# Batch 1's scores in two 64-row bursts, batch 0's output in three parts, and the weight loads in another order, in a one-core attention and mixer kernel

## The chip, the cores and the metric

One core of a Trainium2 chip runs the whole program. The metric is the device time of one execution in microseconds, as the median of repeated runs. Five engines work side by side, each in its own order and held only by semaphores: PE (TensorE, matmuls and transposes), DVE (VectorE), ACT (ScalarE), POOL (GpSimd) and SP (SyncE, which here issues most of the DMAs). POOL issues the weight loads, whose type is changed on the way.

## The reference

Masked attention over 8 batches, 8 heads, 576 positions and 64 features, then two pairs of matmuls:

```
scores = scale * q @ k.T                     # per batch and head
mask: heads 0-3: 0 <= rel < 32;  heads 4-7: 0 <= rel < 128 and rel % 4 == 0
attn = exp(scores) / sum                     # softmax over the allowed keys
x = attn @ v                                 # 576 x 512 per batch
u = x + (relu(x.T @ w_tok1) @ w_tok2).T      # token mixer, 576 -> 256 -> 576
out = u + relu(u @ w_ch1) @ w_ch2            # channel mixer, 512 -> 1536 -> 512
```

Inputs and output are float32 in HBM; the work on the chip is in float16 with float32 sums.

## The kernel before

Batches go through a pipeline. While PE does the channel mixer of batch b (the function `gen_main`), the steps of later batches are put between its matmuls: values and token mixer of batch b+1, scores of batch b+2. `interleave` merges both at build time: each step has a planned time and a cost in planned microseconds, the main generator yields its own costs, and the step with the earliest due time goes next. The result is a fixed order on each engine. The first batches have their times written out by hand at the end of the function (L1006 to L1042).

Names as the profile has them. `l_q`, `l_k`, `l_vn`, `l_vd`, `l_vx`, `l_vt`, `lt` are the float32 loads of a batch (`lt` holds the last 64 rows of q and k); `c_q`, `c_k`, `c_t`, `vv`, `vt` their float16 casts, mostly on POOL. `tp_q`, `tp_k`, `tp_t` are PE transposes into PSUM, copied from there by ACT and DVE into `qz` or `qt` and `kt`, `kr`, `tt`. `sc` and `sm` are score banks; `attp`, `attd` and `attt` the exponentials that ACT writes from them. `av` is the product with v, with the sum of the weights in a 65th column; DVE takes its reciprocal `rec` and writes `xn` (L616, L617). `h1p` and `h1` are the token mixer's hidden layer, `up` and `u16` its result, `tpu` and `uT` that turned over. `gp` and `gt` are the channel mixer's hidden layer in 12 blocks of 128 (L768, weights `w3`), with `gt` L759 for the tail rows; `yp` is its output (L787, weights `w4`), and `o32` the sum that goes to HBM.

Scores come in two forms. In the one-row form (`scores_plain`, `scores_dil`; batches 0 and 1), each head's block is a matmul over 128 rows in which the other head's rows of `qz` are zero, preceded by a matmul of the identity with `veil` (L423) that puts a large negative number where the mask forbids. In the twin form (`scores_twin`, batches 2 to 7), the two heads of a pair use 64 rows each and go side by side; a burst `g` holds two pairs, 24 matmuls on six PSUM banks, and POOL multiplies the exponentials by the mask afterwards. In a batch with twin form the transposes are `bare_steps` (batch 2) or DMAs (batch 3 on).

PSUM has eight banks in three groups: three `main` (gp, yp, gt), two `sc`, three `fl` (transposes, av, h1p, up, tpu). A bank is given anew only when the last reader of its former content is done, so a PE instruction may wait for a copy on ACT or DVE.

Batch 0 has no channel mixer to hide behind: its attention and token mixer run first (L840 to L970). Then come, in program order, the loads of batch 1 behind a small POOL copy that waits for a weight (`gate`, L974), their casts with the last third of `w3` (L984) and all thirds of `w4` (L987 to L990) between, and the loads of batch 2 behind a gate on `w4` (L995). In the channel mixer of batch 0 the output `yp` of a block of 128 rows is summed over all 12 blocks at once (L777 to L804).

Of the kernel before, what the change touches and what calls it, by code (L numbers as in the profile page):

```python
# [20 lines left out]
DM = 512  # L21
# [47 lines left out]
def kernel(  # L69
# [148 lines left out]
    def load_v(b):  # L218
        for step in load_v_steps(b):
            step()  # L220
# [124 lines left out]
    def twinned(b):  # L345
        return b >= 2
# [151 lines left out]
    def scores_twin(b, g):  # L498

        tags = (("sc", 2), ("sc", 2), ("fl", 3), ("fl", 3), ("fl", 3), ("main", 3))  # L500
        if b == 2:
            tags = tags[2:4] + tags[0:2] + tags[4:6]
        ps = [bank(*tags[i], f"sc_{b}_{g}_{i}") for i in range(6)]
        small = ps[4:6]

        def twin(hp, banks, c, keys, queries):
            for h in range(2):
                rows = slice(64 * h, 64 * h + 64)
                n = c.stop - c.start
                nc.tensor.matmul(out=banks[h][:, c], lhsT=keys(rows), rhs=queries(rows), start=True, stop=True)  # L510
# [56 lines left out]
        def mask_tails():  # L567
            t = attt[:, 2 * g:2 * g + 2].rearrange("p a h c -> p (a h) c")[:, :, 64:TW].rearrange(
                "p z (x c) -> p z x c", c=128)[:, :, :, 0:64]
            mult(nc.gpsimd, t, t, tails_seen[g])  # L570

        yield from small_exps(1)
        if b == 2:
            yield from small_exps(0)
        for hp in (2 * g, 2 * g + 1):
            for h in range(2):
                main(hp, h)
                if h and (g or b == 2):
# [3 lines left out]
                yield 0.0  # L582
        if b > 2:
# [145 lines left out]
    def mix_steps(b, t_h1, t_h1b, t_u, t_uT, du=1.0, turn=6.0, gap=2.6):  # L729
# [7 lines left out]
        if turned(b):  # L737
            for t, tail in ((2.0, True), (turn, False))[1 - b % 2:]:
                steps.append((t_u + t * du, 0.0, lambda tail=tail: uT_dma(b, tail)))
            for t, cb in ((0.0, 2), (0.0, 0), (gap, 3), (gap, 1)):  # L740
                steps.append((t_uT + t, 0.0, lambda cb=cb: uT_place(b, cb)))
        else:
            for i, cb in enumerate(CBS):
                steps.append((t_uT + 0.9 * i, 0.28, lambda cb=cb: emit_uT(b, cb)))
        return steps

    def gen_main(b):
# [17 lines left out]
        for mb in range(NMB):  # L765
# [5 lines left out]
            relu(nc.vector if (mb % 2 == 1 if b == 0 else mb % 4 != 3 if b == 1 else mb in (1, 5)) else nc.scalar, gta[:, mb, m0:m0 + 512], p)  # L771
# [5 lines left out]
        for s in ((4, 0, 1, 2, 3) if odd else (0, 1, 2, 3)):  # L777
# [38 lines left out]
    def interleave(main, steps):  # L816
# [3 lines left out]
        while main is not None or steps:  # L820
# [4 lines left out]
            else:  # L825
                try:
                    t += next(main)
# [3 lines left out]
    def warm(n):  # L831

        p = bank("main", 3, "idle_p")
        for _ in range(n):
            nc.tensor.matmul(out=p, lhsT=idle[:, 0:128], rhs=idle, start=True, stop=True)
# [19 lines left out]
    def gate(t, src):  # L855
        nc.gpsimd.tensor_copy(out=t, in_=src)
# [23 lines left out]
    cast_vd(0, 2, nc.gpsimd)  # L880
    load_w3(1)
    cast_vx(0, nc.gpsimd)
# [104 lines left out]
    for i in range(3):  # L987
# [3 lines left out]
    for cast in casts1[12:]:  # L991
        cast()

    new_qk(2)
    gate(l32[(2, "t")][0:1, 0, 0:1], w4[0][0:1, 0:1])  # L995
    for nm in ("q", "k"):
        load_tail(2, nm, nc.sync)
    for h0 in (0, 4):
        for nm in ("q", "k"):
            load_qk(2, nm, h0, h0 + 4, nc.sync)  # L1000
    load_v(2)
# [4 lines left out]
    for b in range(B):  # L1006
        steps = []
        if b == 0:
            steps += score_steps(1, 0, 0, (0.0, 0.7, 1.5),
                                 ((3.0, 5.2), (4.4, 7.0), (7.2, 9.6), (8.6, 11.4)))  # L1010
            va = value_steps(1, 13.4, 0.7)
            steps += va[:4] + [(p + 0.3, c, f) for p, c, f in va[4:]]
            steps += mix_steps(1, 18.0, 20.6, 22.6, 31.4, 1.1)
            steps += at(24.0, 0.3, cast_steps(2))
            bare = bare_steps(2)
            scores2 = score_steps(2, 29.6, 4.4, lag=0.25)
            scores2 = sorted(scores2, key=lambda st: st[0])
            steps += [(t, 0.25, f) for t, f in zip((25.2, 25.9, 27.0, 27.6, 28.2, 34.8, 35.2, 35.6, 36.0), bare)]
            steps += scores2[:10]
            steps += at(34.0, 0.0, [lambda: emit_loads_qk(3)])  # L1020
        elif b == 1:
            va = value_steps(2, 0.0, 1.0)
            steps += [(0.8 + 0.4 * i, c, f) for i, (_, c, f) in enumerate(scores2[10:])]
            steps += [(t, c, f) for t, (_, c, f) in zip((2.2, 3.0, 4.8, 5.6, 8.2, 9.0, 10.4, 11.2), va)]
            steps += mix_steps(2, 7.0, 12.4, 14.6, 24.4, 1.0, 5.6, 0.8)
            casts = cast_steps(3)
            steps += [(6.0 + 0.5 * i, 0.0, casts[i]) for i in (0, 2, 4, 6, 8)]
            steps += [(9.5 + 1.0 * i, 0.0, lambda i=i: cast_qk(3, "q", i, nc.scalar)) for i in range(4)]
            steps += at(11.0, 0.3, casts[9:])
            steps += score_steps(3, 21.0, 4.6, lag=0.1)  # L1030
            steps += at(6.0, 0.0, [lambda: load_v(3)]) + at(20.8, 0.9, load_steps(4))
            steps += at(11.0, 0.9, dma_steps(3)) + at(17.0, 0.4, place_steps(3))
# [40 lines left out]
```

## Time and profile before

| | |
|---|---|
| median of 3 runs | 288.43 us (288.23 to 289.59) |
| the profiled execution | 289.66 us, with a span of 287.8 us |
| PE busy | 276.8 us, 96% of the span |
| ACT, DVE, POOL busy | 134.0, 132.1, 163.0 us |
| granted TensorE clock | 1.00 |
| share of DMA, first 20 us and 20 to 40 us | 1.03 and 1.11 |
| first gp matmul of batch 0 | 28.47 us from the start |
| first yp matmul of batch 0 | 50.38 us |
| first gp matmul of batch 2 | 105.06 us |

A matmul's row has its start and a duration that includes its way through the array (0.38 us for 512 columns), while the next one starts 0.22 us later. So the busy share of PE also covers short waits, and what PE waits is read from the starts of rows.

### The profile page before, as it was taken

The numbers are of one execution on the slowest core, as the hardware profiler recorded it, in microseconds if no ns is written. First come the engines' busy times: TensorE is split into PE (matmuls) and PEld (weight loads), VectorE is DVE, ScalarE is ACT, GpSimd is POOL, SyncE is SP. The second block draws the span as 40 slices with busy tenths as digits, with TensorE's granted clock in tenths as the row PEclk, the third lists the DMA queues.
The fourth block names the chain that finished last, engine by engine and source line by source line (L and its number), as shares of the span: only waits on it lengthen the run. The fifth ranks groups of instructions, "written<-read, shape, count | busy, mean of one in ns | idle before, by whom it ended". The sixth has DMA issues, their size and how long they took to land.

```text
span 287.8 us, 6995 instructions
## 1 busy us (share of the span) xinstructions
PE 276.8 (96%) x2838; PEld 210.9 (73%) x2838; DVE 132.1 (46%) x278; ACT 134.0 (47%) x265; POOL 163.0 (57%) x221
## 2 busy tenths in 40 slices
PE   5879999999999999999999999999999999999995
PEld 2777676888766886698776976797766966886594
DVE  7747658446764236414640164416440274421022
ACT  2854673263543804574447615482546534225500
POOL 6961860478865799449970999279952930000000
PEclk9999999999999999999999999999999999999999
DMA  7999999993999998979888978299974210431023
GB/s 218 263 211 218 283 225 207 320 218 82 328 210 192 264 264 230 139 164 350 226 159 182 330 224 186 57 219 329 193 150 95 85 64 2 91 112 37 0 76 108
DMA packets 105551, 52.63 MB, mean 183 GB/s; under 512 B 73872, under 2 KB 104464, under 8 KB 105520
## 3 DMA queue, kind: packets, MB, share of 16 engines
q1 hardware_dynamic: 101280, 47.07, 67.0%
q0 software_dynamic: 2640, 3.94, 8.0%
q10 hardware_dynamic: 1600, 1.18, 1.4%
q8 instruction: 22, 0.36, 0.6%
q14 instruction: 9, 0.07, 0.1%
HBM read 37.07 MB, written 9.44 MB: 162 GB/s over the span
## 4 chain that ended last, share of the span: by engine, by line
PE 80%; DMA 8%; DVE 3%; POOL 3%; issue 2%; ACT 2%; ACTq 1%; SPq 0%; POOLq 0%; DVEq 0%
PE yp L787 29%; PE gp L768 24%; DMA l_vd<-in_v_dram 4%; PE h1p L627 4%; PE yp L807 3%; DMA l_k<-in_k_dram 3%; PE up L639 3%; PE sc L510 3%; PE gt L759 3%; DVE xn L112 1%; DMA kr<-c_k 1%; PE h1p L625 1%; PE av L608 1%; PE up L650 1%; PE av L603 1%
## 5 line engine op out<-in xcount | busy, mean ns | idle before, releaser
L787 PE MATMUL yp<-w,gt 128*128 128x256 f16 x756 | 87.1, 273 | 0.0
L787 PEld LDWEIGHTS <-gt 128*128 128x128 f16 x768 | 78.6, 106 | 6.5
L106 ACT ACTIVATE gt<-gp 128x512 f16<-128x512 f32 x69 | 41.2, 597 | 76.3 <-PE gp L768 76.0
L768 PE MATMUL gp<-utd,w 128*128 128x512 f16 x144 | 54.7, 380 | 0.0
L768 PE MATMUL gp<-utm,w 128*128 128x512 f16 x144 | 54.6, 379 | 0.0
L768 PEld LDWEIGHTS <-w 128*128 128x128 f16 x384 | 39.2, 114 | 20.3 <-issue 0.5
L797 DVE TENSOR_TENSOR o<-yp,u 128x512 f32<-128x512 f32 x31 | 21.4, 691 | 63.1 <-PE yp L787 58.5
L112 POOL TENSOR_TENSOR attp<-attp,const 128x1280 f16<-128x1280 f16 x12 | 31.4, 2616 | 27.5 <-ACT attp L534 27.4
L112 DVE TENSOR_TENSOR xn<-av,rec 128x320 f16<-128x320 f32 x64 | 31.4, 491 | 2.2
L112 POOL TENSOR_TENSOR attd<-attd,const 128x1024 f16<-128x1024 f16 x12 | 25.3, 2132 | 1.6 <-ACT attd L534 1.6
L768 PE MATMUL gp<-uT,w 128*128 128x512 f16 x96 | 25.8, 379 | 0.0
L108 DVE TENSOR_SCALAR gt<-gp 128x512 f16<-128x512 f32 x27 | 18.5, 686 | 13.6 <-PE gp L768 13.1
L645 DVE TENSOR_TENSOR u<-up,xn 128x512 f16<-128x512 f32 x26 | 17.9, 690 | 7.5 <-PE up L639 7.5
L534 ACT ACTIVATE attp<-sc 128x480 f16<-128x480 f32 (+1 forms) x36 | 16.1, 536 | 7.4 <-PE sc L510 7.4
L102 POOL CAST c_k<-l_k 128x512 f16<-128x512 f32 x29 | 18.0, 628 | 1.9 <-DMA l_k<-in_k_dram 1.7
L102 POOL CAST c_q<-l_q 128x512 f16<-128x512 f32 x27 | 16.8, 629 | 3.1 <-DMA l_q<-in_q_dram 3.1
L616 DVE RECIPROCAL rec<-av 128x5 f32<-128x5 f32 x64 | 12.2, 190 | 13.8 <-PE av L613 13.7
L106 ACT ACTIVATE h<-h1p 128x256 f16<-128x256 f32 x29 | 11.1, 384 | 14.5 <-PE h1p L627 14.1
L399 POOL COPY kt<-kr 128x512 f16<-128x512 f16 x10 | 10.7, 1075 | 9.0 <-DMA kr<-c_k 9.0
L697 ACT COPY utd<-utm 128x512 f16<-128x512 f16 x12 | 12.8, 1135 | 4.1 <-DMA utm<-u 4.1
L102 POOL CAST vv<-l_vn 128x256 f16<-128x256 f32 x32 | 12.0, 420 | 4.3 <-DMA l_vn<-in_v_dram 4.1
L112 POOL TENSOR_TENSOR attt<-attt,const 128x512 f16<-128x512 f16 x12 | 14.0, 1165 | 0.0
(147 smaller groups left out, 459.9 us busy)
## 6 DMA issues: line engine op xcount, KB each, us to landing
out_dram<-o SPq DMA_DIRECT2D x72, 128.0 KB, 3.1
l_q<-in_q_dram SPq DMA_DIRECT2D x15, 512.0 KB, 7.2
l_k<-in_k_dram SPq DMA_DIRECT2D x14, 512.0 KB, 7.1
l_vn<-in_v_dram SPq DMA_DIRECT2D x32, 128.0 KB, 6.6
l_vd<-in_v_dram SPq DMA_DIRECT2D x16, 256.0 KB, 4.6
w<-in_moe_w_ch_dram POOLq DMA_DIRECT2D x6, 512.0 KB, 7.6
lt<-in_q_dram SPq DMA_DIRECT2D x8, 128.0 KB, 4.6
l_vt<-in_v_dram SPq DMA_DIRECT2D x8, 128.0 KB, 4.9
```

The costliest lines, as they stand in the source:

```text
L102: eng.tensor_copy(out=out, in_=in_)
L106: nc.scalar.activation(out=out, in_=in_, func=AF.Relu)
L108: eng.tensor_scalar_max(out=out, in0=in_, scalar1=0.0)
L112: eng.tensor_tensor(out=out, in0=x, in1=y, op=ALU.mult)
L534: nc.scalar.activation(out=out, in_=in_, func=AF.Exp, scale=0.125)
L616: nc.vector.reciprocal(out=rec[:, :, 0], in_=av[:, :, 64])
L627: nc.tensor.matmul(out=p, lhsT=w[:, s, j], rhs=x[:, s, c], start=False, stop=(s == 3))
L645: nc.vector.tensor_tensor(out=u16(b, s), in0=blocks4(p), in1=blocks4(xn[b][:, s]), op=ALU.add)
L697: nc.scalar.copy(out=natural(uTd[:, cb - 2]), in_=uTm[i][:, cb].rearrange("p r m -> p m r"))
L768: nc.tensor.matmul(out=p, lhsT=w3_block(cb, mb), rhs=uT[(b, cb)][0], start=(i == 0), stop=(i == 3))
L787: nc.tensor.matmul(out=p[:, c], lhsT=gta[:, mb, a0:m0 + 512:4] if half else gta[:, mb, a0:a0 + 128], rhs=w4[mb][:, c], start=(mb == 0), st ...
L797: nc.vector.tensor_tensor(out=blocks4(o32), in0=blocks4(p), in1=u16(b, s), op=ALU.add)
```

## The change

- The loads: POOL casts `vt` of batch 0 before it issues the second third of `w3`, and issues the last third right behind it. Batch 1's v loads go in another order. The first third of `w4` is issued behind the casts of batch 1's k; the other two thirds come later, after the first mask and two casts of v. Batch 2's loads no longer wait for `w4`.
- Batch 1 takes the twin form: `bare_steps` for its transposes, two bursts. The second burst has the veil (20 matmuls of 128 columns with the identity), the first is masked by POOL. ACT casts two blocks of `c_q`, DVE casts `vd` and `vx` of batch 1.
- Batch 0's output: blocks 0 to 2 are held in the three `main` banks and summed in three parts of four hidden blocks, with planned times 20.3 and 23.0 for the second and third. Block 3 follows as before. In the hidden layer of batch 0, blocks 0 to 7 are all handed to DVE.
- Six matmuls on `idle` (no result) are put in, three at a time, and the steps of batches 1, 2 and 3 have other times: the scores of batch 2 start behind the first gp of batch 1.

The core of the diff:

```diff
     def twinned(b):
-        return b >= 2
+        return b >= 1
...
         tags = (("sc", 2), ("sc", 2), ("fl", 3), ("fl", 3), ("fl", 3), ("main", 3))
-        if b == 2:
+        if b <= 2:
             tags = tags[2:4] + tags[0:2] + tags[4:6]
...
+        veils = b == 1 and g == 1
...
+        if veils:
+            for p in ps:
+                for r in range(4 if p not in small else 2):
+                    nc.tensor.matmul(
+                        out=p[:, 128 * r:128 * r + 128], lhsT=ident,
+                        rhs=veil[:, BLK + 128:BLK + 256] if p in small else veil[:, 0:128],
+                        start=(r == 0), stop=False)
...
-            relu(nc.vector if (mb % 2 == 1 if b == 0 else mb % 4 != 3 if b == 1 else mb in (1, 5)) else nc.scalar, gta[:, mb, m0:m0 + 512], p)
+            relu(nc.vector if (mb < 8 or mb % 2 == 1 if b == 0 else mb % 4 != 3 if b == 1 else mb in (1, 5)) else nc.scalar, gta[:, mb, m0:m0 + 512], p)
...
+        if b == 0:
+            ps3 = [bank("main", 3, f"yp_{b}_{s}") for s in range(3)]
+            for i in range(3):
+                if i:
+                    yield ("from", (20.3, 23.0)[i - 1])
+                for s, p in enumerate(ps3):
+                    for half in range(2):
+                        c = slice(256 * half, 256 * half + 256)
+                        for mb in range(4 * i, 4 * i + 4):
+                            nc.tensor.matmul(
+                                out=p[:, c],
+                                lhsT=gta[:, mb, s:512:4] if half else gta[:, mb, 128 * s:128 * s + 128],
+                                rhs=w4[mb][:, c], start=(mb == 0 and not half), stop=(mb == NMB - 1 and bool(half)))
...
-        for s in ((4, 0, 1, 2, 3) if odd else (0, 1, 2, 3)):
+        for s in ((4, 0, 1, 2, 3) if odd else (0, 1, 2, 3) if b else (3,)):
...
     cast_vd(0, 2, nc.gpsimd)
+    cast_vx(0, nc.gpsimd)
     load_w3(1)
-    cast_vx(0, nc.gpsimd)
+    load_w3(2)
...
-    load_v(1)
-    casts1 = cast_steps(1)
-    for i in (0, 1):
-        casts1[i]()
-    load_w3(2)
-    for i in (2, 3, 4, 5, 7, 6, 8, 9, 10, 11):
-        casts1[i]()
...
+    load_v(1, (5, 6, 7, 0, 1, 2, 3, 4))
...
+    for i in (0, 1, 3, 2, 4, 6, 8):
+        casts1[i]()
+    load_w4(0)
+
+    def rest1():
+        for i in (9, 10):
+            casts1[i]()
+        load_w4(1)
+        load_w4(2)
+        for i in (11, 12, 13):
+            casts1[i]()
...
         if b == 0:
-            steps += score_steps(1, 0, 0, (0.0, 0.7, 1.5),
-                                 ((3.0, 5.2), (4.4, 7.0), (7.2, 9.6), (8.6, 11.4)))
-            va = value_steps(1, 13.4, 0.7)
...
+            steps += [(t, 0.25, f) for t, f in zip((4.2, 5.4, 7.0, 6.2, 7.6, 11.4, 12.2, 11.8, 12.6), bare)]
+            steps += score_steps(1, 8.9, 4.3, lag=0.25)
+            steps += [(8.6 + 0.6 * i, 0.0, lambda i=i: cast_qk(1, "q", 2 + i, nc.scalar)) for i in range(2)]
+            steps += at(9.0, 0.0, [loads2]) + at(10.8, 0.0, [rest1])
...
+                      zip((16.2, 16.8, 17.5, 18.1, 18.8, 19.4, 21.4, 22.0), (4, 5, 6, 7, 0, 1, 2, 3))]
+            steps += mix_steps(1, 23.2, 20.0, 25.4, 30.2, 1.0, gap_uT=0.8)
+            steps += [(t, 0.0, lambda: warm(3, "sc", 2)) for t in (19.8, 21.3)]
...
-            steps += scores2[:10]
...
         elif b == 1:
             va = value_steps(2, 0.0, 1.0)
...
+            steps += scores2
```

More of the change, by code (lines that the diff above doesn't have):

```diff
@@ L216, in load_v_steps, with load_v @@
         return steps
-    def load_v(b):
-        for step in load_v_steps(b):
-            step()
+    def load_v(b, order=range(8)):
+        steps = load_v_steps(b)
+        for i in order:
+            steps[i]()
     def load_steps(b):
@@ L504, in scores_twin @@
         small = ps[4:6]
+        veils = b == 1 and g == 1
         def twin(hp, banks, c, keys, queries):
+            ends = c.stop == (512 if banks is not small else 256)
             for h in range(2):
                 rows = slice(64 * h, 64 * h + 64)
-                n = c.stop - c.start
-                nc.tensor.matmul(out=banks[h][:, c], lhsT=keys(rows), rhs=queries(rows), start=True, stop=True)
+                nc.tensor.matmul(out=banks[h][:, c], lhsT=keys(rows), rhs=queries(rows),
+                                 start=not veils, stop=ends or not veils)
+        if veils:
[5 more added lines that the diff above has]
+                        start=(r == 0), stop=False)
         for j in range(2):
@@ L577, in scores_twin @@
                 main(hp, h)
-                if h and (g or b == 2):
+                if h and b == 1 and hp == 0:
+                    mask(0)
+                    mask_tails(0)
+                elif h and (b == 2 or (g and b > 2)):
                     mask(hp)
@@ L582, in scores_twin @@
                 yield 0.0
+        if b == 1 and g == 0:
+            mask(1)
+            mask_tails(1)
         if b > 2:
```

79 lines of the change are left out of this document (48 added, 31 removed).

## The prediction

> **What bounds the kernel now.** I read the page first: the busy line and the chain that ended last.
>
> ```profile
> PE 276.8 (96%) x2838; PEld 210.9 (73%) x2838; DVE 132.1 (46%) x278; ACT 134.0 (47%) x265; POOL 163.0 (57%) x221
> ...
> PE 80%; DMA 8%; DVE 3%; POOL 3%; issue 2%; ACT 2%; ACTq 1%; SPq 0%; POOLq 0%; DVEq 0%
> ```
>
> PE sets the end; no other engine is over 57%. So a change is worth the PE work that it removes, plus the waits of PE that it removes, less those that it makes. Next, PE's timeline, at three places that both kernels have, and PE's rows in the list of waits:
>
> ```profile
> 28.47 3.48 PE L768 MATMUL gp<-uT,w 128*128 128x512 f16 x14
> ...
> 50.38 0.82 PE L787 MATMUL yp<-w,gt 128*128 128x256 f16 x6
> ...
> 105.06 0.38 PE L768 MATMUL gp<-utd,w 128*128 128x512 f16 x1
> ```
>
> ```profile
> PE av L611 <- POOL vt L102: 1.2, 1, 1.2
> ...
> PE h1p L625 <- DVE xn L112: 0.4, 1, 0.4
> PE sc L510 <- POOL kt L399: 0.2, 1, 0.2
> ```
>
> From batch 2's first gp (105.06) on, the order is the old one, so the change is decided before it. For the work in between I need the pitch of a matmul, from chain and timeline:
>
> ```profile
> 122.45 0.75 PE sc L510 x24
> ...
> 126.58 0.67 PE sc L510 x24
> ...
> 138.66 0.90 PE gt L759 x16
> ...
> 258.13 3.45 PE gp L768 x16
> ...
> 273.76 9.17 PE yp L787 x84
> ```
>
> ```profile
> 34.30 0.23 PE L423 MATMUL sc<-veil,const 128*128 128x160 f16 x1
> ...
> 34.44 0.23 PE L423 MATMUL sc<-veil,const 128*128 128x160 f16 x1
> ...
> 42.89 0.19 PE L423 MATMUL sm<-veil,const 128*128 128x64 f16 x1
> ...
> 43.09 0.19 PE L425 MATMUL sm<-qz,kt 128*128 128x64 f16 x1
> ```
>
> That is 0.216 for 512 columns, 0.109 for 256, 0.056 for 128, 0.07 for 160 (two steps in 0.14), 0.03 for 64 (seven steps in 0.20). Between 28.47 and 105.06 stand 108 matmuls of 512 columns with their 4 in up (112: 24.2), 268 of 256 (29.2), 140 transposes and gt of 128 (7.8), 120 av of 65 columns (3.6), batch 1's scores (4.9, below) and four bursts (2.8): 72.5 of 76.6. PE waits only 4.1 here, in many pieces; some 1.0 of it are pieces that the new order keeps, 3.1 belong to the old order and go.
>
> **The change part by part.** All times are microseconds.
>
> *The head.* POOL's order around `vt`, before and then after (`w3_1`, `w3_2` are thirds of the first weight):
>
> ```order
> L102 CAST vv0_69<-l_vd_0_123 128x4x2x64 x2
> L860 DMA w3_1_85<-in_moe_w_ch1_dram 128x4x512
> L102 CAST vt0_71<-l_vx_0_124 128x4x64
> L883 DMA w1t1_80<-in_moe_w_tok1_dram 64x256
> L885 COPY w2p_0_82<-w2_81 128x512
> L885 COPY w2p_1_83<-w2_81 128x512
> ```
>
> ```order
> L102 CAST vv0_69<-l_vd_0_123 128x4x2x64 x2
> L102 CAST vt0_71<-l_vx_0_124 128x4x64
> L908 DMA w3_1_85<-in_moe_w_ch1_dram 128x4x512
> L908 DMA w3_2_86<-in_moe_w_ch1_dram 128x4x512
> L932 DMA w1t1_80<-in_moe_w_tok1_dram 64x256
> L934 COPY w2p_0_82<-w2_81 128x512
> L934 COPY w2p_1_83<-w2_81 128x512
> ```
>
> The cast moves ahead of one DMA issue, and one issue more stands ahead of the `w2p` copies. In the trace:
>
> ```profile
> 19.08 0.63 POOL L102 CAST vv<-l_vd 128x512 f16<-128x512 f32 x1 [1.91 <-DMA l_vd<-in_v_dram]
> 19.65 0.74 POOL L860 DMA_DIRECT2D w<-in_moe_w_ch_dram  x1
> 20.38 0.42 POOL L102 CAST vt<-l_vx 128x256 f16<-128x256 f32 x1
> ...
> 21.25 1.25 POOL L885 COPY w2p<-w 128x512 f16<-128x512 f16 x2
> ```
>
> ```profile
> 25.96 0.38 PE L949 MATMUL up<-h,w2p 128*128 128x256 f16 x2
> ```
>
> PE's 1.2 wait for `vt` ends one issue earlier: -0.7, and all that follows up to gp with it. The `w2p` copies end 0.8 later, near 23.3, and PE's first use of them at 25.96 becomes 25.3: still covered, nothing.
>
> *PE's work.* Batch 1's scores were 24 matmuls of 160 columns, 40 of 128, 32 of 64: 1.7 + 2.2 + 0.9 = 4.9. Two bursts cost 0.75 + 0.67, the veil of the second 20 x 0.056 = 1.1: 2.5. That is -2.3. Six idle matmuls: +1.3. The thirds of yp and the transposes are as many as before. Together -1.0.
>
> *New waits, first stretch (to the second third of yp).* They come from order and banks. DVE's order at batch 1's keys, before and after (`gt` is the relu, `kt`, `kr` key copies):
>
> ```order
> L108 TENSOR_SCALAR gt_93<-gp_0_3_677 128x512
> L314 COPY kt_65<-tp_k_1_0_695 128x512
> L102 COPY qz_64<-tp_q_1_1_701 64x576 x2
> L102 COPY kt_65<-tp_q_1_1_701 128x64
> L314 COPY kt_65<-tp_k_1_1_724 128x512
> L108 TENSOR_SCALAR gt_93<-gp_0_5_713 128x512
> ```
>
> ```order
> L386 COPY kt_65<-tp_k_1_0_688 128x512
> L108 TENSOR_SCALAR gt_93<-gp_0_7_685 128x512
> L386 COPY kt_65<-tp_k_1_1_697 128x512
> L108 TENSOR_SCALAR gt_93<-gp_0_9_767 128x512
> L388 COPY kr_67<-tp_k_1_2_810 128x512
> L389 COPY kt_65<-tp_k_1_2_810 128x128
> L388 COPY kr_67<-tp_k_1_3_817 128x512
> L389 COPY kt_65<-tp_k_1_3_817 128x128
> ```
>
> The key copies of a whole burst now stand close together, and the burst needs both. Durations, and how closely ACT follows a burst that PE left at 61.19:
>
> ```profile
> L108 DVE TENSOR_SCALAR gt<-gp 128x512 f16<-128x512 f32 x27 | 18.5, 686 | 13.6 <-PE gp L768 13.1
> ...
> L385 DVE COPY kt<-tp_k 128x512 f16<-128x512 f16 x2 | 1.4, 686 | 0.4 <-PE tp_k L378 0.4
> L387 DVE COPY kr<-tp_k 128x512 f16<-128x512 f16 x2 | 0.8, 420 | 0.2 <-PE tp_k L378 0.2
> ...
> L388 DVE COPY kt<-tp_k 128x128 f16<-128x128 f16 x2 | 0.6, 280 | 0.0
> ```
>
> ```profile
> 61.38 0.38 ACT L534 ACTIVATE attp<-sc 128x256 f16<-128x256 f32 x1 [1.79 <-PE sc L510]
> ...
> 62.46 1.53 ACT L534 ACTIVATE attp<-sc 128x480 f16<-128x480 f32 x3
> 63.81 0.76 ACT L100 COPY uT<-tpu 128x640 f16<-128x640 f16 x1
> ```
>
> Four small exponentials take 1.08 from start to start, a large one 0.45; an engine starts 0.2 behind PE. The second key copy ends 0.2 + 3 x 0.65 = 2.1 after the first tp_k; PE is there after half a gp, a tp_k, a gp and half a burst, 1.8: wait 0.3. All three `fl` banks are held by the burst, so the next transposes wait for ACT's exponentials, behind a cast and four small ones: 0.2, 0.3, and 0.1 for a veil. The last tp_k takes over the bank of the one just ahead of it: 0.2 + 0.42 + 0.28, about 0.9. Together 1.5 to 1.8; I take 1.8.
>
> Then the heads. DVE needs 0.63 a head:
>
> ```profile
> 45.05 0.49 DVE L112 TENSOR_TENSOR xn<-av,rec 128x320 f16<-128x320 f32 x1
> ...
> 45.68 0.49 DVE L112 TENSOR_TENSOR xn<-av,rec 128x320 f16<-128x320 f32 x1
> ```
>
> Before, a gp of 0.43 or more stood between two heads. Now heads 5, 6, 7, 0, 1 follow each other at 0.17 to 0.27, and with three banks the last three wait 0.2, 0.45 and 0.35. The first head waits 0.3 for POOL, whose order has the mask of the first burst ahead of the last v cast. Together 1.3. Bounds of the stretch: 1.4 to 4.
>
> *New waits, second stretch (to 105).* tpu and the transposes of batch 2 now follow each other without yp between: one waits for a bank that ACT empties with the 0.76 copy (0.5), others 0.1 and 0.3 for DVE. Batch 2's first burst comes behind gp 0 of batch 1, and its last tp_k waits for eight exponentials and a copy: 0.2 + 1.1 + 1.8 + 0.6 against 3.2 of PE work: 0.5. Values of head 0 and 1 then wait for POOL's masks and for ACT: 0.7.
>
> ```profile
> L112 POOL TENSOR_TENSOR attp<-attp,const 128x1280 f16<-128x1280 f16 x12 | 31.4, 2616 | 27.5 <-ACT attp L534 27.4
> ...
> L112 POOL TENSOR_TENSOR attt<-attt,const 128x512 f16<-128x512 f16 x12 | 14.0, 1165 | 0.0
> ```
>
> Both h1p pairs come half a gp behind their last head, where DVE needs 0.97 for one and 1.6 for two: 0.5 each. Together 3.1, bounds 1.5 to 4.
>
> *The loads.* w4's first third is issued near 38, when the last load of k, pushed back by up to 3 by w3's last third, is cast; the other two behind the first mask, its tails and two casts of v (2.6 + 0.6 + 0.8 from about 41.3), near 45.5 and 46; PE wants them near 45, 53 and 57.5. Rows of before on them, and on a v load issued right behind a third of w3 (issued at 30.76):
>
> ```profile
> 39.20 1.61 POOL L988 DMA_DIRECT2D w<-in_moe_w_ch_dram  x3
> ```
>
> ```profile
> DMA to landing us min/median/max: 5.5/7.4/10.6
> ```
>
> ```profile
> DMA to landing us min/median/max: 7.8/7.8/7.8
> ```
>
> ```profile
> 38.85 0.41 POOL L102 CAST vv<-l_vn 128x256 f16<-128x256 f32 x1 [2.39 <-DMA l_vn<-in_v_dram]
> ```
>
> The first two answers are for the three thirds of w4 and for the third of w3. The w3 part landed at 38.6, and the v load, a quarter of its size, right after it and not before: that looks like order of issue. But w4's thirds landed some 2.4 and 3.7 apart, the last with batch 2's loads beside it, so loads also share. The Trainium skill ("DMA: Bandwidth & Descriptors", section "Queues, rings and completion order") says that each DMA engine takes turns between the queue rows that have work, packet by packet. By that rule w4 isn't held back by q and k, and the sum stands as below; by order of issue it is the first rival. I take sharing: the second third lands 5.5 + 1.3 after 45.5, near 52.3, and costs nothing; bounds 0 to 1.9. Batch 1's c_t and c_q come up to 3 later behind w3's last third, about when PE wants them: 0, at most 0.9.
>
> *The sum.* -0.7 - 1.0 + 3.1 + 3.1 - 3.1 (old waits) = +1.4. It is a difference within one profiled execution (289.66, of which 287.8 is span); that one lies 1.2 above the median, 288.43, on which I lay it: 289.8, rounded down to 289.7 as neighbouring waits take from each other.
>
> **The rivals.** *The second weight arrives late (slower).* SP has issued four loads of batch 2, 512 KB each, when POOL reaches the second third of w4.
>
> ```profile
> 53.56 0.61 POOL L102 CAST c_q<-l_q 128x512 f16<-128x512 f32 x1 [0.58 <-DMA l_q<-in_q_dram]
> 55.13 0.61 POOL L102 CAST c_k<-l_k 128x512 f16<-128x512 f32 x1 [0.96 <-DMA l_k<-in_k_dram]
> ```
>
> They land 1.5 apart. In order of issue they are through near 52, the third lands near 54.6, and PE has waited since 52.9: +1.7, so 291.4. For it: the v load above. It decides from the point where the landing passes 53.
>
> *The new waits are no more than the old (faster).* If ACT and DVE run ahead enough that 3.1 of new waits replace 3.1 of old ones, the head and the shorter scores remain: 286.7. For it: waits of 0.3 shift each other, and the old order, as dense, has just 4.1. Against: the bank behind the last tp_k, 0.63 a head and the h1p pairs are bound by durations; the 0.4 of h1p in the list of waits is such a case.
>
> **How the numbers follow.** 0.5% is 1.4, about what a measurement here tells from no change: 287.0 and 289.9 are its ends. My forecast has 0.50, with an own range of 288.7 to 290.7: 0.31 within the ends and 0.19 above. The late weight has 0.16, all above. Waits as before: 0.27, of it 0.21 below 287.0. What is left, 0.07, is spread: 0.01, 0.03, 0.03. So faster 0.22, same 0.40, slower 0.38. The range from 286.6 to 291.6 takes in both rivals' times.
>
> **What would show it.** In the profile after: the first gp near 27.8; two bursts of 24 matmuls more and two rows of `idle_p` x3 near 52; PE waiting for DVE before the last tp_k of batch 1 (0.9) and among the heads of batch 1; the second third of yp near 53; batch 2's first gp near 106.5. I am wrong if the second third starts before 51.5 or after 54.5, or if batch 2's first gp comes before 104.5.

## The result and the profile after

The change makes the kernel slower: 293.5 us (median of four; 291.81 to 297.87) against 288.36, ratio 1.0156 with a 95% interval of 1.0125 to 1.0186. Six more runs, later, gave 1.0182 (1.0151 to 1.0213). One run of each set (297.9 and 297.8) had a lower clock and is left out of the ratio, as are, further down, two of e1 (the profiled one among them) and one each of e3, e7, e13 and e14. The forecast was 289.7.

The profiled execution of after took 292.5 (span 290.73), that of before 289.66 (287.82). The page of after, its busy line and the engines' shares of the chain that ended last:

```profile
PE 277.3 (95%) x2816; PEld 209.5 (72%) x2816; DVE 133.5 (46%) x279; ACT 134.2 (46%) x267; POOL 166.0 (57%) x217
...
PE 78%; DMA 11%; POOL 3%; ACT 2%; DVE 2%; issue 1%; ACTq 1%; SPq 1%; POOLq 0%
```

PE is as busy as before; what grew is the share of the DMA in the chain, from 8% to 11%. PE's timeline of after, at the places that the prediction named (start, length, group, and in brackets the idle time ahead with what ended it):

```profile
26.67 4.56 PE L787 MATMUL gp<-uT,w 128*128 128x512 f16 x19
...
53.75 1.03 PE L813 MATMUL yp<-w,gt 128*128 128x256 f16 x8 [1.26 <-DMA w<-in_moe_w_ch_dram]
...
107.38 0.38 PE L787 MATMUL gp<-utd,w 128*128 128x512 f16 x1
```

So 28.47 became 26.67 for the first gp, and 105.06 became 107.38 for batch 2's first. The difference in span, +2.91, is -1.80 up to the first gp, **+4.12 from there to batch 2's first gp** (76.59 to 80.71), +0.20 to batch 3's (28.70 to 28.90) and +0.39 behind it, all behind the last output's landing. The second third of yp starts at 53.75, inside the bounds of the forecast, but for the wrong reason: PE stood there and waited. The list of PE's waits from the first gp to batch 2's:

```profile
PE yp L813 <- DMA w<-in_moe_w_ch_dram: 1.3, 1, 1.3
PE av L622 <- ACT attt L546: 0.8, 1, 0.8
PE tp_k L379 <- DVE kt L389: 0.8, 1, 0.8
PE h1p L644 <- DVE xn L112: 0.8, 2, 0.4
PE av L622 <- DVE xn L112: 0.4, 2, 0.2
PE tp_k L379 <- ACT qt L384: 0.3, 1, 0.3
PE tp_q L379 <- ACT uT L100: 0.3, 1, 0.3
```

Six of the seven rows are waits that the prediction priced, five at about their sizes and one (batch 1's heads, `av` from `xn`) at less. The first is the one it priced at 0. The trace of the loads that write `w`, for the two thirds that POOL issues at 44.4 and 45.0:

```profile
  PE yp L813: 1.3, 1
...
DMA to landing us min/median/max: 9.3/10.2/11.2
```

They take 9.3 and 11.2 and land at 53.7 and 56.1; the thirds of before took 5.5 to 10.6. The DMA view tells why. Three stretches of 1.5 after the issue at 44.4 (q1 carries SP's loads, q0 POOL's; packets, MB, share of 16 engines), from 47, from 48.5 and from 50:

```profile
q1 hardware_dynamic: 527, 0.52, 109.7%
...
q0 software_dynamic: 61, 0.25, 82.0%
q1 hardware_dynamic: 155, 0.15, 33.3%
...
q0 software_dynamic: 65, 0.27, 87.2%
q1 hardware_dynamic: 65, 0.06, 15.4%
```

Until 48.5 not one packet of w4 moves (nor in e9, a second profile of after): the loads that SP issued first, of tails, q and k, go through alone. From then on the two queues take turns, 65 packets against 65, as the Trainium skill's rule has it ("DMA: Bandwidth & Descriptors", section "Queues, rings and completion order"). So both rules that the prediction set against each other held here, one after the other: order of issue for 4 us, then turns. The DMA engines are full throughout; the windows of after show it (the column ahead of the last is their share):

```profile
26.67:53.75 27.08, 24.08 (x256) 15.77 (x254) 16.98 (x38) 11.53 (x25) 17.14 (x24) 1.00 1.14 269
...
51.20:54.60 3.40, 2.13 (x30) 1.65 (x29) 1.70 (x5) 0.00 (x0) 1.56 (x3) 1.00 1.07 233
```

### The profile page after: what moved, and what is told of

It is laid out like the page before. It is cut to its first block, busy times and chain, and to the rows that moved or that the text cites. A ratio compares the mean times of both kernels' runs of the same rounds, so it can differ in the third digit from the quotient of the medians.

```text
span 290.7 us, 6955 instructions
## 1 busy us (share of the span) xinstructions
PE 277.3 (95%) x2816; PEld 209.5 (72%) x2816; DVE 133.5 (46%) x279; ACT 134.2 (46%) x267; POOL 166.0 (57%) x217
## 4 chain that ended last, share of the span: by engine, by line
PE 78%; DMA 11%; POOL 3%; ACT 2%; DVE 2%; issue 1%; ACTq 1%; SPq 1%; POOLq 0%
PE yp L834 26%; PE gp L787 25%; PE up L658 4%; PE gt L778 4%; PE yp L854 4%; PE h1p L646 4%; DMA w<-in_moe_w_ch_dram 3%; DMA l_k<-in_k_dram 3%; PE sc L513 3%; DMA l_q<-in_q_dram 3%; DMA l_vx<-in_v_dram 2%; PE yp L813 2%; PE h1p L644 1%; ACT attp L546 1%; PE av L622 1%; PE up L669 1%
## 5 line engine op out<-in xcount | busy, mean ns | idle before, releaser
L834 PE MATMUL yp<-w,gt 128*128 128x256 f16 x684 | 77.6, 273 | 0.0
L834 PEld LDWEIGHTS <-gt 128*128 128x128 f16 x696 | 71.4, 106 | 5.5
L106 ACT ACTIVATE gt<-gp 128x512 f16<-128x512 f32 x65 | 39.0, 600 | 64.9 <-PE gp L787 64.6
L112 POOL TENSOR_TENSOR attp<-attp,const 128x1280 f16<-128x1280 f16 x14 | 36.6, 2612 | 38.0 <-ACT attp L546 28.2
L787 PE MATMUL gp<-utm,w 128*128 128x512 f16 x144 | 54.6, 379 | 0.0
L844 DVE TENSOR_TENSOR o<-yp,u 128x512 f32<-128x512 f32 x28 | 19.4, 692 | 61.1 <-PE yp L834 50.8
L108 DVE TENSOR_SCALAR gt<-gp 128x512 f16<-128x512 f32 x31 | 21.3, 688 | 12.4 <-PE gp L787 12.0
L546 ACT ACTIVATE attp<-sc 128x480 f16<-128x480 f32 (+1 forms) x42 | 18.7, 538 | 14.1 <-PE sc L513 14.0
L787 PE MATMUL gp<-uT,w 128*128 128x512 f16 x96 | 24.7, 380 | 0.0
L112 POOL TENSOR_TENSOR attt<-attt,const 128x512 f16<-128x512 f16 (+1 forms) x14 | 15.2, 1085 | 0.0
L546 ACT ACTIVATE attd<-sc 128x512 f16<-128x512 f32 x28 | 14.4, 613 | 0.0
```

Source lines behind the costliest of these rows:

```text
L106: nc.scalar.activation(out=out, in_=in_, func=AF.Relu)
L108: eng.tensor_scalar_max(out=out, in0=in_, scalar1=0.0)
L112: eng.tensor_tensor(out=out, in0=x, in1=y, op=ALU.mult)
L546: nc.scalar.activation(out=out, in_=in_, func=AF.Exp, scale=0.125)
L787: nc.tensor.matmul(out=p, lhsT=w3_block(cb, mb), rhs=uT[(b, cb)][0], start=(i == 0), stop=(i == 3))
L834: nc.tensor.matmul(out=p[:, c], lhsT=gta[:, mb, a0:m0 + 512:4] if half else gta[:, mb, a0:a0 + 128], rhs=w4[mb][:, c], start=(mb == 0), st ...
```

## The experiments

Theory **loads without slack** (in the first expectations, "late weight"): the order's own waits are about what was forecast; the new order wants the second weight 4 us earlier against the first gp (yp starts at 44.25, 17.6 behind it; before, 21.9) and its second third comes late. Rival **order and banks**: the waits of the new order make the loss, and PE's wait for the weight covers others of its size. Their time against before is a ratio with its interval. The table holds what PE's timeline shows of each profiled execution: the first gp, the stretch to batch 2's first gp (the one in dispute), and from there to batch 3's. Over the stretch in dispute two executions of one kernel differ by 1.1 (before) and 0.4 (after).

| kernel | first gp | to batch 2 | to batch 3 | ratio |
|---|---|---|---|---|
| before | 28.47 | 76.59 | 28.70 | |
| before again (e8) | 26.66 | 77.66 | 28.70 | |
| vt first (e4) | 26.83 | 76.51 | 28.70 | 0.9997 (0.9983-1.0012) |
| after | 26.67 | 80.71 | 28.90 | 1.0156 (1.0125-1.0186) |
| after again (e9) | 26.73 | 80.33 | 28.88 | 1.0182 (1.0151-1.0213) |
| w4 early (e1) | 27.14 | 84.53 | 33.83 | 1.0316 (1.0276-1.0356) |
| no idle (e2) | 26.93 | 82.60 | 29.24 | 1.0162 (1.0122-1.0203) |
| both (e3) | 27.78 | 82.02 | 29.50 | 1.0283 (1.0242-1.0323) |
| w4, then batch 2 (e5) | 27.30 | 79.63 | 33.21 | 1.0174 (1.0136-1.0212) |
| thirds amid heads (e6) | 28.54 | 79.39 | 29.41 | 1.0145 (1.0118-1.0172) |
| fewer waits (e7) | 26.98 | 78.94 | 29.28 | 1.0105 (1.0083-1.0128) |
| batch 4's loads early (e10) | 26.63 | 81.19 | 31.12 | 1.0269 (1.0247-1.0292) |
| that, loads by need (e11) | 27.99 | 79.29 | 31.15 | 1.0211 (1.0186-1.0236) |
| fewer waits, w4 at start (e12) | 38.02 | 75.98 | 28.82 | |
| loads by need (e13) | 26.77 | 76.90 | 29.89 | 1.0005 (0.9987-1.0024) |
| and q1 later (e14) | 26.79 | 76.79 | 29.55 | 1.0044 (1.0025-1.0064) |
| after, w4 at start (e15) | 37.10 | 79.20 | 33.18 | |
| before, w4 at start (e16) | 39.10 | 76.36 | 28.69 | |
| by need, burst earlier (e17) | 26.82 | 76.53 | 28.75 | 1.0012 (0.9995-1.0029) |
| and sc banks (e18) | 26.74 | 76.95 | 28.99 | 0.998 (0.9958-1.0002) |

**The weight early (e1).**

```
     load_w4(0)
+    load_w4(1)
+    load_w4(2)
...
-        load_w4(1)
-        load_w4(2)
```

> The kernel after, with all three thirds of the second weight issued by POOL behind each other where now only the first is (near 37.4); the casts and masks behind them stay in order. Theory 'late weight': in the profile of after PE waits 1.43 for the second third, issued at 44.4 and landed at 53.7. Issued near 38 it lands near 47, and that wait goes. What is late next is DVE, which finishes heads 2 and 3 of batch 1 near 53.4 where PE would want them for h1p near 53.0: 0.6 comes back, 0.2 more is gained as POOL's last v cast comes earlier (POOL idles 2.25 ahead of its first mask, so the two issues cost it nothing). In sum 1.0 to 1.1 less than after, ratio to before 1.012; up to 2 less (1.009) if the weight comes later still in the timed runs than in the profiled one. Rival 'order and banks' (the loss is made of the waits of the new order, and PE's wait for the weight covers one for DVE of the same size): the ratio stays at 1.0145 to 1.0156.

The wait for w4 went, and 4.0 came in its place. PE's waits, how long v's tail took that SP issued 0.2 behind the first third, and the windows (length, then PE's busy time; the third column from the right is the granted clock):

```profile
PE av L632 <- POOL vv L102: 4.0, 1, 4.0
...
DMA to landing us min/median/max: 12.2/12.2/12.2
...
48.10:51.50 3.40, 0.24 (x3) 0.24 (x3) 0.01 (x1) 0.00 (x0) 0.90 (x2) 1.00 1.12 257
51.50:54.90 3.40, 3.25 (x42) 2.58 (x41) 2.94 (x10) 0.00 (x0) 3.40 (x3) 0.50 1.10 349
...
130.00:133.40 3.40, 1.12 (x26) 0.86 (x27) 0.00 (x0) 0.00 (x0) 3.05 (x5) 1.00 0.88 176
133.40:136.80 3.40, 3.40 (x18) 2.43 (x17) 0.00 (x0) 3.06 (x8) 0.46 (x1) 0.50 0.95 188
```

Both theories missed. A third of w4 gained is a load of v lost, since the engines are full; and a stretch of 3.4 in which PE is idle enough is followed by 3.4 at half clock. That is a price which no part of the prediction had. The two low stretches start 81.9 apart, 24 times 3.41, as if the clock were set anew at fixed times. It fits the Trainium skill ("TensorE: Matmul & The Clock Gate", section "Part 1: The HAM clock gate (the "warmup" mystery)"), which gives a free-running window of 3413 ns.

**Without the idle matmuls (e2), and with both edits (e3).**

```
-            steps += [(t, 0.0, lambda: warm(3, "sc", 2)) for t in (19.8, 21.3)]
```

> The kernel after without the two rows of three idle matmuls (1.29 of PE work, near 49.4 and 51.1). Theory 'late weight': PE comes to the second third of yp 0.8 to 1.3 earlier and waits that much longer for its weight, which still lands near 53.7: within 0.2 of after, ratio to before 1.015 to 1.0165. Rival 'PE work and order' (PE sets this stretch): 0.8 to 1.3 less than after, ratio 1.011 to 1.013.

> Both edits at once. Theory 'late weight': with the weight there, DVE's heads (0.63 each) set the stretch: heads 2 and 3 come 0.8 earlier to PE but wait for banks, h1p half 1 waits 0.5 for head 7: some 0.5 less than with the early weight alone, ratio to before 1.010 to 1.011. Rival 'PE work and order': the same as without idle matmuls alone, 1.011 to 1.013.

For e2 the theory's number came: 1.29 of PE work less, and the same time. But its profiled execution (295.0) shows a longer wait (1.9) and then half clock:

```profile
50.90:54.30 3.40, 1.52 (x27) 1.18 (x25) 2.27 (x8) 0.38 (x1) 2.52 (x5) 1.00 1.06 229
54.30:57.70 3.40, 3.40 (x17) 2.43 (x17) 0.00 (x0) 0.39 (x1) 0.50 (x1) 0.50 1.10 300
```

PE was busy for 1.52 of 3.40 here and for 2.13 in the row of after above, which stays at full clock. The Trainium skill ("TensorE: Matmul & The Clock Gate", section "Why this matters for your kernels") advises against idle gaps over some 3 us. Here one of 1.9 with others beside it was enough, so the busy share of the stretch tells more than its longest gap. In this execution the idle matmuls were missed. That they keep after at full clock is not shown: two of e2's six executions have a mean clock of 0.994, which is one stretch of 3.4 at half clock (1.7 of some 294), and so have two of after's ten. e3 is e1 again, with the wait for v's tail at 2.9, outside both expectations.

**The head (e4, e8).** e4 is before with the cast ahead of one issue; e8 is before unchanged.

```
     cast_vd(0, 2, nc.gpsimd)
+    cast_vx(0, nc.gpsimd)
     load_w3(1)
-    cast_vx(0, nc.gpsimd)
```

> The kernel before with one edit: POOL's cast of vt stands ahead of its issue of the first weight's second third (the third third stays where before has it). Prediction's term: PE's wait for vt ends 0.7 earlier and all behind it moves by that: ratio to before 0.9975. Rival 'the head gives all that the two profiles show' (first gp at 28.47 before, 26.67 after): 1.8 less, ratio 0.994. Rival 'cover': what comes behind (the first weight's thirds, the loads of batch 1) is late next and nothing is gained: 0.999 to 1.001.

> The kernel before, unchanged, for a second profile. In the profile shown the first gp of before stood at 28.47, with the vt cast moved ahead (a run of its own) at 26.83, and yet the two take the same time (0.9997). Theory 'a slow head in that one execution': here the first gp stands near 27.0, and the span from there to batch 2's first gp is again 76.6 within 0.3. Rival 'the cast gains 1.6 at the head and loses it behind': the first gp stands near 28.4 again.

The cast's move is worth nothing (0.9997). PE's waits of e8 from 14 to 30, POOL's row of the cast there, and PE's first gp:

```profile
PE sc L425 <- DVE kt L314: 0.2, 1, 0.2
PE up L949 <- ACT h L106: 0.2, 1, 0.2
...
18.59 0.41 POOL L102 CAST vt<-l_vx 128x256 f16<-128x256 f32 x1 [0.78 <-DMA l_vx<-in_v_dram]
...
26.66 3.48 PE L768 MATMUL gp<-uT,w 128*128 128x512 f16 x14
```

The 1.2 that PE waited for `vt` isn't there. In the execution first shown, half of `vd` landed at 19.0 and held POOL for 1.9 (its row is in the prediction); here both halves are there by 16.5, and the cast waits for its own load whichever side of the issue it stands on. Theory "a slow head" holds for the first gp, but not for the stretch: e8's is 1.1 longer. Batch 1's first q lands 2.9 behind the first gp there, and 1.6 behind it in the execution first shown and in e4; PE then waits for casts of q and k (0.5 in its list).

**The weight ahead of batch 2's loads (e5), yp amid the heads (e6), fewer waits (e7).**

```
         load_w4(2)
+        loads2()
...
         new_qk(2)
+        gate(l32[(2, "t")][0:1, 0, 0:1], w2p[1][0:1, 0, 0:1])
...
-            steps += at(9.0, 0.0, [loads2]) + at(10.8, 0.0, [rest1])
+            steps += at(10.8, 0.0, [rest1])
```

e6 leaves the idle matmuls out and lays the second third earlier; e7 adds a bank:

```
-                    yield ("from", (20.3, 23.0)[i - 1])
+                    yield ("from", (18.0, 21.6)[i - 1])
...
-            p = bank("fl", 3, f"tp_{nm}_{b}_{hp}", FP16)
+            p = bank(*(("sc", 2) if (nm, hp) == ("k", 3) else ("fl", 3)), f"tp_{nm}_{b}_{hp}", FP16)
```

e6 also spreads the heads (16.2 to 21.2) and moves the first h1p pair to 20.9; e7 moves batch 2's heads 0 to 3 by 0.4 to 0.9 and its h1p and up steps by 0.6 to 1.1.

> The kernel after, with batch 2's loads on SP held back until POOL has issued the second weight's second and third third (near 45.5, as late as in the kernel before); POOL's order of casts, masks and w4 stays, with one small copy more. In the early-weight run v's tail (issued by SP 0.2 behind the first third) landed at 50.5 behind all three thirds and PE waited 4.2 for it; here it keeps its place. Theory 'late weight': of the 1.43 that PE waited at the second third of yp nothing is left, as the third lands near 48.5; 0.6 comes back at h1p, which waits for DVE's heads 2 and 3: 0.8 less than after's profile (292.5), and no stretch of 3.4 at half clock any more: ratio to before 1.010 to 1.012. Rival 'order and banks': PE's wait turns into others of the same size, here or at batch 2's transposes, whose loads come later: 1.0135 to 1.0156.

> As the last, and without the six idle matmuls, and with the second third of yp laid between heads 7, 0, 1, 2, 3 and the first h1p pair, where after has heads close together. Theory 'late weight': once the weight is there by 48.5, yp fills what DVE needs for a head (0.63), so that the 0.96 of waits between heads, the 1.29 of idle matmuls and h1p's 0.6 go: 2.2 to 2.8 less than the last, ratio to before 1.002 to 1.005. Rival 'order and banks': DVE and ACT set this stretch whatever PE does between: not under 1.009.

> As the last, with the last key transposes of batches 1 and 2 in a bank of their own (the sc pair in place of fl), batch 2's heads 0 to 3 a gp or half a gp later, and its h1p and up steps 0.6 to 1.1 later. If the waits that PE shows in the profile of after are each worth their length: 0.97 + 0.50 (last tp_k), 1.0 (first head of batch 2, behind its second burst), and most of 0.55 + 0.56 (h1p) go: 2.0 to 2.9 less than the last, ratio 0.992 to 0.998, the first version ahead of before. If such waits only move on to the next step: within 0.5 of the last, 1.001 to 1.005.

In e5 the disputed stretch became 1.1 shorter, near what the theory said (0.8), and the time did not. In the profiled execution, the longest of six (296.4), batch 4's keys came late and half clock followed. The other five (292.6 to 294.3) have mean clocks of 0.998 to 1.000, so no whole stretch at half clock; what held them isn't shown.

```profile
PE sc L513 <- POOL kt L400: 2.5, 2, 1.5
...
124.89:128.29 3.40, 1.37 (x28) 1.08 (x29) 0.00 (x0) 0.23 (x1) 3.04 (x5) 1.00 0.88 173
128.29:131.70 3.41, 3.41 (x19) 2.42 (x17) 0.19 (x1) 2.84 (x8) 0.71 (x1) 0.50 0.92 185
```

e6's stretch is 0.2 shorter where 2.2 to 2.8 were expected, and e7's time another 0.4%, between its two expectations. In e7's list the waits for DVE and ACT that were aimed at are gone or small, and PE, earlier at yp, waits for its weight twice:

```profile
45.66 2.35 PE L813 MATMUL yp<-w,gt 128*128 128x256 f16 x20 [1.24 <-DMA w<-in_moe_w_ch_dram]
...
50.35 1.03 PE L813 MATMUL yp<-w,gt 128*128 128x256 f16 x8 [0.91 <-DMA w<-in_moe_w_ch_dram]
```

So the waits of order and banks can be taken away, but part of the gain is lost at the next late load: the two rows make 2.2, where after has one wait of 1.3.

**After again, batch 4's loads, loads by need, w4 at the start (e9 to e12).** e10 puts `load_steps(4)` at 20.8; e11 has this besides (the last piece is `rest1`: v's tail, w4, then the plain v):

```
-    load_v(1, (5, 6, 7, 0, 1, 2, 3, 4))
+    load_v(1, (5, 6, 7, 4, 0, 1, 2, 3))
...
-    for i in (0, 1, 3, 2, 4, 6, 8):
+    for i in (0, 1, 3, 2, 4):
         casts1[i]()
     load_w4(0)
+    for i in (6, 8):
+        casts1[i]()
+    load_w4(1)
...
+        casts1[13]()
         load_w4(2)
         loads2()
-        for i in (11, 12, 13):
+        for i in (9, 10, 11, 12):
             casts1[i]()
```

> The kernel after, unchanged, for a second profile and six more times. So far: PE waits 1.43 for the second third of yp; where such a wait and what stands beside it leave a 3.4 stretch of PE under about 0.36 of its columns, the next 3.4 run at half clock (1.7 to 3.4 more); so one run in some is 3 to 5 longer. Theory 'loads without slack': the second third lands between 53.5 and 55 and PE waits 1.2 to 2.5 for it; ratio 1.013 to 1.017. Rival 'order and banks': the wait there is 0 to 1 here, and the time is the same.

> The version with fewer waits, with one more edit: batch 4's loads are put into SP's order where the kernel before has them (20.8 in the list of batch 1), not behind the transposing DMA of batch 2's u (25.6), at which SP stands 3 to 3.6 in its queue. In the run with batch 2's loads held back the key copies of batch 4 came late (kr landed at 124.7, PE waited 2.5 and ran its next 3.4 at half clock: 33.2 from batch 2's first gp to batch 3's, against 28.7 in before). Theory 'loads without slack': that stretch goes from 29.3 to 28.7, no execution loses more there: ratio 1.007 to 1.009 against 1.0105. Rival 'order and banks': unchanged, 1.010 to 1.011; or slower, if the transposing DMA behind six loads comes late.

> As the last, with the loads in the order in which PE and DVE want them: v's tail ahead of the plain v, the first third of w4 issued while POOL would wait for batch 1's last k (34.6), the second right behind the last k cast (near 37.5), the last third behind v's tail cast. Theory 'order of the loads': the waits for w4 (1.41 at the first third of yp, 1.08 at the second) go, and v comes late enough to do no harm: 1.5 to 2.5 less than the last, ratio 0.999 to 1.003. Rival 'bytes': the DMA engines are full from 22 to 60 whatever the order, so what w4 gains is waited for at v (heads near 46 to 50) or at batch 2's q: within 0.7 of the last, not under 1.006.

> The version with fewer waits, with all of w4 loaded at the very start, ahead of all else, to take 1.5 MB out of the stretch between the first gp and batch 2's first gp; the head pays for it (first gp some 5 to 8 later), so only the stretch is read. Theory 'loads without slack': the stretch goes from 78.9 to 76.0 to 76.8 (the waits of 1.41 and 1.08 for w4 go, and batch 2's q is cast 0.3 to 0.5 earlier), as short as in before or shorter. Rival 'order and banks': 78.3 to 79.

e9 waits for w4 as after did (1.2), and five of its six executions reach from 292.2 to 295.1. e12's stretch is 75.98: with w4's bytes out of it, 3.0 of e7's 78.94 go, a little more than the theory said. e10 made a new loss. SP's row of the transposing DMA, and PE's row of batch 2's first gp that wants it:

```profile
98.68 4.76 SPq L706 DMA_TRANSPOSE utm<-u x1
...
107.82 0.38 PE L787 MATMUL gp<-utd,w 128*128 128x512 f16 x1 [2.69 <-ACT attt L546]
```

Behind six loads its issue stood 4.76, to 103.4 (the last of the six landed at 102.7); in after it stood 3.10. ACT's copies of it, which the row puts down to another ACT instruction, started at 105.5 against 102.3 in after, and half clock followed (31.12):

```profile
45.95:49.36 3.41, 1.35 (x23) 1.15 (x23) 2.20 (x8) 0.36 (x1) 3.41 (x4) 1.00 0.95 181
47.41:50.82 3.41, 2.13 (x39) 1.87 (x36) 2.17 (x8) 0.00 (x0) 2.54 (x2) 1.00 1.04 203
105.43:108.84 3.41, 0.59 (x2) 0.21 (x2) 0.44 (x1) 3.36 (x6) 0.00 (x0) 1.00 0.78 206
108.84:112.25 3.41, 2.97 (x23) 1.70 (x23) 0.76 (x3) 1.75 (x4) 3.37 (x2) 0.50 1.10 351
```

PE was busy for only 1.35 of the first row's 3.41, and the clock stayed full. Counted back from 108.84 in steps of 3.41, the clock's own stretches are those that end at 47.4 and 50.8, and PE was busy for 2.13 of the second. So it matters where a wait lies against these stretches, and one kernel can lose clock in one execution and not in the next.

e11 has the same loss at batch 2's first gp, and no wait for w4 in its list; so the two had to be told apart.

**Order of the loads, or bytes (e13, e14); the order without the loads (e15, e16).** e13 is e11 with `load_steps(4)` back at 25.6. e14 transposes batch 2's second q and k between the halves of its first gp. e15 and e16 load w4 ahead of all else, which costs the head over 10 us.

> The loads by need, with batch 4's loads back behind the transposing DMA of batch 2's u, where after has them. Theory 'order of the loads': the run with both edits lost 2.95 before batch 2's first gp and 2.3 behind it to that DMA, which SP issued behind six loads; without that 76.3 are left from the first gp to batch 2's first gp and 28.8 to 29.3 to batch 3's: span 286 to 287, ratio 0.996 to 1.000. Rival 'bytes': the time comes back at v, at batch 2's q or at batch 4's keys (half clock among it): 1.006 or more.

> As the last, with the second q and k of batch 2 transposed between the halves of its first two gp in place of ahead of them, and the first burst 1.0 later. In the profiles of the last four versions PE waits 0.89 and 0.38 at these two transposes (for DVE's uT copy, whose bank they take). If that wait is worth its length: 0.8 to 1.2 less than the last, ratio 0.992 to 0.997; if it only moves on (to the bursts or batch 2's heads): the same within 0.4.

> The kernel after, with all of w4 loaded at the very start; only the stretch from the first gp to batch 2's first gp is read (80.7 and 80.3 in the two profiles of after). Theory 'loads without slack': the wait of 1.4 for the second third goes, 0.6 comes back at h1p: 79.3 to 79.9; against 76.5 to 77.7 of before that leaves 2 to 3 for the order itself, as the prediction had it (+2.1). Rival 'the loads are all of it': 77 or less.

> The kernel before, with all of w4 loaded at the very start, for the same stretch (76.6, 77.7, and 76.5 with the vt cast first). If before waits for no load in it: 76.3 to 76.7. If its loads cost it something too: 75.5 or less.

e13 against e7: the same instructions on PE in the same order, the loads (and with them POOL's casts) in another, and the ratio goes from 1.0105 to 1.0005. Its stretch is 76.90; what is left is at batch 4's keys:

```profile
26.77 4.56 PE L787 MATMUL gp<-uT,w 128*128 128x512 f16 x19
...
103.67 0.38 PE L787 MATMUL gp<-utd,w 128*128 128x512 f16 x1
...
PE sc L513 <- POOL kt L400: 0.9, 1, 0.9
```

Rival "bytes" falls. The prediction's own question, what the order costs without the loads, is answered by e15 less e16:

```profile
37.10 4.77 PE L787 MATMUL gp<-uT,w 128*128 128x512 f16 x20
...
116.30 0.38 PE L787 MATMUL gp<-utd,w 128*128 128x512 f16 x1
```

```profile
39.10 3.48 PE L768 MATMUL gp<-uT,w 128*128 128x512 f16 x14
...
115.46 0.38 PE L768 MATMUL gp<-utd,w 128*128 128x512 f16 x1
```

79.20 less 76.36 is +2.84, from one execution each. The rows of PE's list over this stretch are 3.7 in e15 and 0.8 in e16: 2.9 more, and with 1.0 of work less 1.9. The other 0.9 is in waits too short for a row, or has another cause; the lists don't show it. e12, with w4 out of the way in the same manner, stands at 75.98: what e5 to e7 change (the hold on batch 2's loads, the idle matmuls, steps and a bank) takes all of it away again. e14's stretch was 0.1 shorter, and its time 0.4% longer, which neither expectation had: those waits moved on (to the first burst's keys and to gp, 0.4 each in its list).

**Batch 3's burst earlier (e17), and banks (e18).**

```
-            steps += mix_steps(2, 12.9, 18.4, 20.4, 28.6, 1.0, 5.6, 0.8)
+            steps += mix_steps(2, 12.9, 18.2, 20.0, 28.6, 0.9, 5.6, 0.8)
...
-            steps += score_steps(3, 25.8, 4.6, lag=0.1)
+            steps += score_steps(3, 24.3, 4.4, lag=0.1)
```

e18, besides:

```
-            p = bank(*(("sc", 2) if (nm, hp) == ("k", 3) else ("fl", 3)), f"tp_{nm}_{b}_{hp}", FP16)
+            p = bank(*(("sc", 2) if (nm, hp) == ("k", 3) or b == 2 and nm == "q" and hp < 2 else ("fl", 3)), f"tp_{nm}_{b}_{hp}", FP16)
```

> The loads by need, with batch 3's first burst 1.3 earlier (its up steps 0.9 in place of 1.0 apart), the transposing DMA of batch 2's u still ahead of all of batch 4's loads. POOL's masks and its casts of batch 4 come 1 to 1.3 earlier, so its keys do: if that is what sets batch 4's first burst, the wait of 0.9 to 1.1 there goes (29.9 from batch 2's first gp to batch 3's becomes 28.8) and no execution falls to half clock there: ratio to before 0.996 to 0.999. If the loads of batch 4 set it, whenever POOL is free: 1.000 to 1.002.

> As the last, with the first two query transposes of batch 2 in the sc banks, which stand empty there, in place of taking an fl bank from a u transpose (PE waits 0.44 and 0.89 for that, and 0.38 right behind). If the waits are worth their length: 1.0 to 1.7 less than the last, ratio 0.991 to 0.995. If the copies of DVE and ACT set this place (gp needs the last u copy): 0 to 0.5 less, 0.995 to 0.999.

In e17's profile the wait at the keys is gone, as one of the two expected (29.89 to 28.75), and none of its twelve executions has a mean clock under 0.997, where one of e13's had 0.987; its time is still that of before (1.0012) and not the 0.996 to 0.999 that was to go with it. e18 is the shortest of all that were run, 0.998, but its interval reaches 1.0002: no version is shown to beat before. Its list has 0.5 at the transposes of q and k, e17's 1.2 (0.7, 0.3 and 0.2); but 0.4 at that of the tails and 0.8 for POOL's masks, where e17 has none and 0.4, and its stretch is no shorter.

## Why the prediction was wrong, point by point

**The step that failed** is "I take sharing: the second third lands 5.5 + 1.3 after 45.5, near 52.3, and costs nothing". It took 9.3, not 6.8, and cost 1.3 (1.4 between the starts of rows), though it was issued 1.1 earlier than assumed (44.4). That cost is within the bounds given there, 0 to 1.9, but the sum took 0. The 5.5 came from a third that had the engines nearly to itself; here two loads of 512 KB and more stood ahead of it in a full stretch, and turns began only as the second of those came to its end. Rival 1 named the wait and its sign, with order of issue (54.6); the landing (53.7) lies between the two rules. Two more terms were mis-sized, the head and the new waits, by 0.7 each, and so rival 1's 291.4 is too low as well.

**The head, -0.7:** measured 0 (e4, whose interval leaves at most 0.5). It was a wait of one execution, caused by a load that came 2.6 later than in the other profiled one. The -1.8 of the two profiles is that as well, not the change.

**PE's work, -1.0:** the count is right (22 matmuls fewer in all), but taking out the 1.29 of idle matmuls gained nothing, as PE waits behind them anyway (e2).

**New waits, +3.1 and +3.1 for 3.1 old ones:** with the work this was +2.1 over the stretch; e15 and e16 give +2.84 for the order alone, 0.7 more. Most mechanisms are in the list of after, near their sizes: last tp_k 0.8 (0.9 forecast), the two h1p pairs 0.8 (1.0), batch 2's first head 0.8 (0.7), heads of batch 1 0.4 (1.0). Where the rest of the 2.84 sits, the lists don't show.

**The sum** in measured terms is 0 + 2.8 + 1.3 = 4.1, which is the stretch in the first two profiles. That it fits to the tenth is luck: between the second two (e9 less e8) the stretch grew by 2.7. On a usual execution of before, 288.4, 4.1 makes 292.5, the time of after's profiled execution. The ratios make it 292.9 to 293.6. The rest is in executions without a profile: 293.8, 294.5 and 295.1, at mean clocks of 0.998 to 1.000. Late loads at batch 4's keys, as in e5, could do this; it wasn't seen in an execution of after, so it stays open.

**Laying the sum on the median** hid an error of its own: the profiled execution of before was 1.2 longer than the median, most likely because of the very wait that the sum took away.

**What no part priced:** that a late load, together with the waits around it, can halve the clock of the next 3.4.

## What to carry to other kernels

When an edit brings the use of a load forward within a stretch in which the DMA engines are full, put all the loads of that stretch in the order of need and count the bytes ahead of each; here that was worth 1% (e7 to e13), and moving only the late one made it worse (e1). A wait that stands in a single profiled execution is no term of a sum until a second execution shows it. Where PE is busy for 1.5 or less of 3.4 us, price the chance that the next 3.4 run at half clock: they did in e1, e2, e5 and e10, and did not where that time lay across two of the clock's stretches.

## What the runs showed of the hardware

- After 3.4 us in which PE was busy for 0.24, 0.59, 1.12, 1.37 or 1.52, the next 3.4 ran at a granted clock of 0.50; after 2.13 (after and e10) it did not. In e2 the longest single wait before it was 1.9. In e1 two such stretches start 24 times 3.41 apart, and in e10 1.35 of 3.41 that lay across two of them cost no clock.
- POOL's loads of w4 move in packets of 4 KB at 0.27 MB in 1.5 us beside one packet of 1 KB each of SP's, 219 GB/s in all; SP's loads of q and k alone ran at 349.
- The transposing DMA of batch 2's u kept SP at its issue for 4.76 us behind six loads in e10, and for 3.10 in after, where outputs stood ahead. What makes it that long isn't shown.
